# The first loads of a decode kernel: both halves of the gate weights at once, x behind them

## The chip, the cores and the metric

The kernel runs on one core of one Trainium2 chip. The metric is the device time of one execution in microseconds (us), as the median of several runs. A core has five engines that run side by side: TensorE (PE in the profile; PEld is its weight load), VectorE (DVE), ScalarE (ACT), GpSimd (POOL) and SyncE (SP). Loads from device memory (HBM) are issued by SP and by ACT, each into a queue of its own, and are moved by 16 DMA engines.

## The reference

One decode step of an attention block, gated by a gated linear unit, for 8 sequences with one token each (D = 512), 32 query heads, 8 key/value heads of 128, and a window of the last 2048 of 8192 cached positions. All inputs are bf16. The unit has F = 1792 hidden columns.

```python
def _A_ref(x, k_cache, v_cache, wq, wo):        # attention over the window
    W = min(4096, max(256, Sk // 4))             # 2048
    q = (x @ wq).reshape(B, Sq, Hq, Dh).transpose(0, 2, 1, 3)
    k = jnp.repeat(k_cache[:, :, Sk - W:, :], rep, axis=1)
    v = jnp.repeat(v_cache[:, :, Sk - W:, :], rep, axis=1)
    scores = jnp.einsum("bhqd,bhkd->bhqk", q, k) * (Dh ** -0.5)
    o = jnp.einsum("bhqk,bhkd->bhqd", _softmax(scores, axis=-1), v)
    return o.transpose(0, 2, 1, 3).reshape(B, Sq, Hq * Dh) @ wo

def _B_ref(x, w_gate, w_up, w_down):             # gated linear unit
    h = _sigmoid(x @ w_gate) * (x @ w_up)
    return h @ w_down

xn = _layernorm(A_x)
return A_x + _A_ref(xn, ...) * _silu(_B_ref(xn, ...))
```

## The kernel before, in words

The kernel reads some 81 MB, nearly all of it once. It has three stages: the gated unit and the queries at the start, the attention over 8 batch entries, and the output product at the end.

**Loads.** Two pools hold what arrives: `kpool` with 5 buffers and `vpool` with 4. A list `todo` gives the order of all loads: gate weights (`want_first`), up weights, down weights (one part of them in a tile `wd_part` of its own, L179 to L190, after the query weights), query weights in two tiles, then K tiles and V tiles of 2 MB each with V three tiles behind K, and last the output weights `wo` in five pieces. `pump` (L110) issues loads from the head of the list as long as the pool of the next one has room; `free` (L116) gives a buffer back and pumps again. Nearly all loads go to SP's queue (`q0`); ACT's queue (`q1`) gets one half of the gate weights and the small load of `x4_sb`. Each engine's instructions run in the order of the program, and a load's issue stands in that order too, so an issue that has to wait holds back all issues behind it.

**The first loads.** `want_first` (L147) issues three things. `x_bf` is x as 8 rows of 512 values, for the normalisation. The gate weights are one tile with four rows of `w_gate` for each partition; rows 0 and 1 go to ACT's queue, rows 2 and 3 to SP's. `x4_sb` is x once more, as four column blocks of 128 values in every fourth partition (32 pieces of 256 bytes); it is cleared by GpSimd at L144, and it is read once, at the very end (L750), where x is added to the result.

**The gated unit.** x is cast, its mean and variance are taken, and it is normalised (L223 to L236; the square root is on ACT), turned by TensorE (L247) and written to `xnT_sb` (L254). Then DVE clears and prepares other tiles (L259 to L280). TensorE multiplies with the gate weights (`hidden`, L295, 16 matmuls), ACT takes the sigmoid (L308), TensorE multiplies with the up weights (16 more), DVE forms the product `h_sb` (L312) and turns it (L320). The down product (L348) has 13 matmuls with `wd_sb` and 3 with `wd_part`. L357 to L375 sum its four blocks and form `gg_sb`, the gate's silu, with a sigmoid on ACT (L371).

**Queries and attention.** TensorE forms q with the query weights (L385); ACT and DVE copy it (L399, L401), and it is turned into `qm_sb`. From then on each K tile is turned on TensorE (L481), copied by DVE (L486) and multiplied with q (L500); maxima, exponentials (L548 on ACT), the turned probabilities (L571) and the products with V (L597) of earlier batch entries lie between. A K or V buffer is free, and the next load can be issued, when the last instruction that reads it is done.

**The end.** The output product (L719, L733) takes the pieces of `wo` as they land; DVE multiplies with `gg_sb` (L748) and adds `x4_sb` (L750), and SP and ACT store one half each (L752).

Of the kernel before, what the change touches and what calls it, by code (L numbers as in the profile page):

```python
# [10 lines left out]
def kernel(  # L11
# [14 lines left out]
    P = 128  # L26
# [54 lines left out]
    q0, q1 = nc.sync, nc.scalar  # L81
# [55 lines left out]
    x_bf = work.tile([B, D], bf16, name="x_bf")  # L137
# [3 lines left out]
    S = Z // B  # L141
    NB = D // P
    x4_sb = work.tile([P, P], bf16, name="x4_sb")
# [2 lines left out]

    def want_first():  # L147
        t = vpool.tile([P, KT, F], bf16, name="wg_sb", tag="v")
        q0.dma_start(out=x_bf[:], in_=A_x.flatten_outer_dims())
        for q, r0 in ((q1, 0), (q0, KT // 2)):  # L150
            q.dma_start(
                out=t[:, r0 : r0 + KT // 2, :],
                in_=B_w_gate.rearrange("(p r) n -> p r n", r=KT)[
                    :, r0 : r0 + KT // 2, :
                ],
            )
        q1.dma_start(
            out=x4_sb[::S, :],
            in_=A_x.flatten_outer_dims().rearrange("b (j c) -> j b c", c=P),
        )  # L160
        for r in range(KT):
            weights[("wg_sb", r)] = t[:, r, :]

    later("v", want_first)
    want_rows("wu_sb", B_w_up, "v", KT, 0, KT)

# [38 lines left out]
    for t0, t1 in ((0, 12), (12, KS), (KS, 26), (26, 30), (30, RT)):  # L205
# [11 lines left out]
        out=perm[:].rearrange("k (l p) -> k l p", l=G),  # L217
        in_=ident[:].rearrange("k (p l) -> k l p", l=G),
# [13 lines left out]
        out=rstd[:], in_=mv[:, 1:2], func=AF.Sqrt, bias=eps_t[:], scale=1.0  # L232
# [4 lines left out]
        out=xn_bf[:],  # L237
# [8 lines left out]
    for kt in range(KT):  # L246
        nc.tensor.transpose(  # L247
            out=xnT_ps[:, kt, :],
            in_=xn_bf[:].rearrange("b (p kt) -> b kt p", kt=KT)[:, kt, :],
# [11 lines left out]
    for t in p_buf:  # L261
# [7 lines left out]
        out=own_q[:], in_=ident_f[:].rearrange("k (h q) -> k q h", q=NDQ), axis=AX.X  # L269
# [3 lines left out]
        out=sel_z[:], in_=ident_f[:].rearrange("k (j z) -> k z j", z=Z), axis=AX.X  # L273
# [4 lines left out]
    for p0, n, x0, x1, s0, a in PARTS:  # L278
        for x in range(x0, x1):
            nc.vector.tensor_copy(  # L280
                out=sel_part[:, x, p0 : p0 + n].rearrange("k (a e) -> k a e", a=a),
                in_=ident[:, s0 : s0 + n * (x1 - x0)].rearrange(
                    "k (e x a) -> k x a e", x=x1 - x0, a=a
                )[:, x - x0],
# [6 lines left out]
    def hidden(name):  # L291
# [21 lines left out]
        out=h_sb[:].rearrange("k t p -> k p t"),  # L313
# [7 lines left out]
        out=hT_sb[:].rearrange("k t z -> k (t z)"),  # L321
        in_=h_sb[:].rearrange("k t p -> k (t p)"),
# [23 lines left out]
    for t, (h, w) in enumerate(down):  # L346
        j = t % NB
# [25 lines left out]
    free("v")  # L373
    gg_sb = work.tile([P, P], f32, name="gg_sb")
    nc.vector.tensor_tensor(out=gg_sb[:], in0=sigb[:], in1=b_ps[:], op=ALU.mult)  # L375

# [23 lines left out]
    for x in range(Hkv // JQ):  # L402
        for r in range(rep):
            nc.tensor.transpose(  # L404
                out=qT_ps[:, x, r, :], in_=q_bf[:, x, r, :], identity=ident[:]
            )
        nc.vector.tensor_copy(
            out=qm_sb[:, :, x * JQ : (x + 1) * JQ, M0 : M0 + rep],
            in_=qT_ps[:, x].rearrange("d r (j z) -> d z j r", z=Z)[:, ::S],
# [11 lines left out]
    for i in range(NQ):  # L421
        nc.vector.tensor_copy(
            out=turn_rows[:].rearrange("k (i j l r) -> k i j l r", i=NQ, j=NJ, l=G)[
                :, i
            ],
            in_=ident[:].rearrange("k (l j i r) -> k i j l r", i=NQ, j=NJ, l=G)[:, i],
        )
        nc.vector.reduce_sum(
            out=sel_den[:, i * Hh : (i + 1) * Hh].rearrange("k (l r) -> k l r", l=G),
            in_=ident_f[:].rearrange("k (l j i r) -> k i l r j", l=G, j=NJ, i=NQ)[:, i],  # L430
            axis=AX.X,
        )
    for e in range(2):
        nc.vector.reduce_sum(
            out=sel_out[:, e, :].rearrange("k (i h) -> k i h", i=NQ),
            in_=ident_f[:].rearrange(
                "k (i m e h) -> k e i h m", i=NQ, m=NJ // 2, e=2
            )[:, e],
# [9 lines left out]
        out=sel_res[:],  # L448
# [6 lines left out]
        out=sel_sum[:], in_=sel_den[:].unsqueeze(2).to_broadcast([P, Hq, NDQ])  # L455
# [261 lines left out]
    for t in range(KS):  # L717
        j = t % NB
# [32 lines left out]
    for x, q in enumerate((q0, q1)):  # L751
        q.dma_start(  # L752
            out=out.flatten_outer_dims().rearrange("b (j c) -> j b c", c=P)[
                x * NB // 2 : (x + 1) * NB // 2
            ],
            in_=y_bf[x * HP : (x + 1) * HP : S, :],
# [31 lines left out]
```

## Time and profile before

| | |
|---|---|
| median of 3 runs | 199.88 us (199.76 to 199.95) |
| the profiled execution | 199.75 us |
| its span, first to last instruction | 198.0 us |
| bytes read from HBM | 81.02 MB, 409 GB/s over the span |
| queue of SP (q1): packets, MB | 6224, 80.10 |
| queue of ACT (q10): packets, MB | 198, 0.93 |
| busy: PE, DVE, ACT, POOL | 155.6, 122.6, 37.7, 2.7 us |

All times in the profile count from the first instruction of the span. A row of the timeline gives start, duration, engine, line, operation, the tile written and the tile or tensor read; in brackets stands how long the engine was idle before it and what released it. "SPq" and "ACTq" are the issues of loads on the two queues; an issue is not the transfer, which comes later. The strip on the page cuts the span into 40 slices of 4.95 us; a digit is a busy share in tenths, 9 being 90% or more. The name `x_sb` in the profile is the tile `x4_sb` with its number left out. Windows give the busy time of each engine in a stretch of time, the granted clock of TensorE, the mean busy share of the 16 DMA engines (it can pass 1, since a packet counts where it starts) and the rate in GB/s.

### The profile page before, as it was taken

How to read it: one execution, taken by the hardware profiler on the slowest of the kernel's cores; microseconds unless marked ns; L12 is line 12 of the kernel's file. 1: busy time of each engine (PE TensorE's matmuls, PEld its weight loads, DVE VectorE, ACT ScalarE, POOL GpSimd, SP SyncE). 2: the span in 40 equal slices, each digit the busy share in tenths (PEclk: the TensorE clock that was granted, in tenths of full speed). 3: DMA queues.
4: the chain of work that ended last, by engine and by line, in shares of the span. 5: the costliest groups of instructions: out<-in, count | busy, mean ns of one | idle time of the engine just before them, and what ended most of it. 6: DMA issues, size and time to landing. Idle time of an engine off the chain costs nothing.

```text
span 198.0 us, 4774 instructions
## 1 busy us (share of the span) xinstructions
PE 155.6 (79%) x2133; PEld 105.6 (53%) x2133; DVE 122.6 (62%) x234; ACT 37.7 (19%) x91; POOL 2.7 (1%) x11
## 2 busy tenths in 40 slices
PE   0434038999979999999798869996999997888552
PEld 0111014877766677656565646674667665566421
DVE  3773001999978679758675927686767874852301
ACT  3300011000620520150024000600060033082010
POOL 5000000000000000000000000000000000000000
PEclk9999999999999999999999979997899999999985
DMA  6999999999999999999999999999999999999980
GB/s 209 446 430 434 426 425 427 434 440 429 424 420 430 430 427 437 430 430 420 430 427 425 427 440 430 422 434 424 424 430 440 420 430 437 427 420 425 420 336 10
DMA packets 6441, 81.32 MB, mean 411 GB/s; under 512 B 782, under 2 KB 918, under 8 KB 1558
## 3 DMA queue, kind: packets, MB, share of 16 engines
q1 hardware_dynamic: 6224, 80.10, 95.0%
q10 hardware_dynamic: 198, 0.93, 1.4%
q8 instruction: 16, 0.26, 0.5%
q14 instruction: 3, 0.02, 0.0%
HBM read 81.02 MB, written 0.01 MB: 409 GB/s over the span
## 4 chain that ended last, share of the span: by engine, by line
DMA 57%; PE 36%; ACT 3%; DVE 1%; SPq 1%; issue 1%
DMA k_sb<-in_A_k_cache_dram 32%; PE kT_ps L481 19%; DMA wo_sb<-in_A_wo_dram 11%; DMA wd_part<-in_B_w_down_dram 10%; PE o_ps L597 6%; PE s_ps L500 5%; DMA wg_sb<-in_B_w_gate_dram 3%; ACT p_buf L548 2%; PE pT_ps L571 2%; PE q_ps L385 1%; SPq L99 1%; ACT L548 1%; PE qT_ps L404 1%; PE fin_ps L733 1%; PE b_ps L361 0%
## 5 line engine op out<-in xcount | busy, mean ns | idle before, releaser
L486 DVE COPY kT_sb<-kT_ps 128x1024 bf16<-128x1024 bf16 x128 | 85.4, 687 | 30.2 <-PE kT_ps L481 29.5
L481 PE MATMUL kT_ps<-perm,k_sb 128*128 128x128 bf16 x1024 | 78.0, 225 | 8.2 <-DMA k_sb<-in_A_k_cache_dram 8.2
L481 PEld LDWEIGHTS <-k_sb 128*128 128x128 bf16 x1024 | 61.1, 101 | 28.0 <-issue 16.7
L597 PE MATMUL o_ps<-v_sb,pT_sb 128*32 128x256 bf16 x512 | 40.3, 279 | 1.2 <-DVE o_sb L618 0.9
L597 PEld LDWEIGHTS <-pT_sb 128*32 128x32 bf16 x512 | 22.1, 97 | 10.3 <-issue 3.8
L500 PE MATMUL s_ps<-kT_sb,qm_sb 128*32 128x512 bf16 x256 | 26.0, 396 | 0.7 <-DVE kT_sb L486 0.7
L548 ACT ACTIVATE p_buf<-s_ps,nb 32x512 bf16<-32x512 f32 x32 | 21.8, 680 | 0.5
L541 ACT COPY nb<-m_ps 128x1 f32<-128x1 f32 x8 | 1.3, 160 | 88.3 <-PE m_ps L535 88.3
L571 PE MATMUL pT_ps<-turn_rows,p_buf 128*128 128x128 bf16 x128 | 11.0, 230 | 1.5 <-ACT p_buf L548 1.5
L564 DVE COPY pT_sb<-pT_ps 128x1024 bf16<-128x1024 bf16 x14 | 9.6, 687 | 3.9 <-PE pT_ps L571 3.9
L571 PEld LDWEIGHTS <-p_buf 128*128 128x128 bf16 x128 | 9.4, 151 | 3.4 <-ACT p_buf L548 2.1
L500 PEld LDWEIGHTS <-qm_sb 128*32 128x32 bf16 x256 | 6.6, 93 | 7.7 <-issue 1.4
L613 ACT ACTIVATE o_odd<-o_ps,own_col 128x128 f32<-128x128 f32 x8 | 2.9, 368 | 26.8 <-PE o_ps L597 26.7
L375 DVE TENSOR_TENSOR gg_sb<-sigb,b_ps 128x128 f32<-128x128 f32 x1 | 0.3, 289 | 12.2 <-ACT sigb L371 12.2
L348 PE MATMUL w_ps<-wd_part,hP_sb 52*32 52x512 bf16 (+1 forms) x3 | 0.6, 597 | 8.3 <-DMA wd_part<-in_B_w_down_dram 8.3
L548 ACT ACTIVATION_READ_ACCUMULATOR p_buf<-s_ps,nb 32x1 f32 x32 | 5.9, 184 | 0.0
L515 DVE TENSOR_REDUCE st<-s_ps 128x1 f32<-128x512 f32 x8 | 5.5, 682 | 0.5 <-PE s_ps L500 0.5
L348 PEld LDWEIGHTS <-hP_sb 52*32 52x32 bf16 (+1 forms) x3 | 0.1, 98 | 9.2 <-issue 9.2
L247 PE MATMUL xnT_ps<-ident,xn_bf 8*128 8x8 bf16 x4 | 0.3, 174 | 5.8 <-DVE xn_bf L236 5.8
L640 DVE SCALAR_TENSOR_TENSOR own<-m_ps,inv,own_q 128x128 f32<-128x128 f32 x8 | 2.8, 345 | 3.1 <-PE m_ps L631 3.1
L618 DVE SCALAR_TENSOR_TENSOR o_sb<-o_ps,own_col,o_odd 128x128 f32<-128x128 f32 x8 | 2.7, 341 | 3.1 <-ACT o_odd L613 3.1
L295 PE MATMUL h_ps<-wu_sb,xnT_sb 128*32 128x448 bf16 x16 | 1.7, 572 | 3.4 <-DMA wu_sb<-in_B_w_up_dram 3.4
(80 smaller groups left out, 67.1 us busy)
## 6 DMA issues: line engine op xcount, KB each, us to landing
k_sb<-in_A_k_cache_dram SPq DMA_DIRECT2D x16, 2048.0 KB, 29.9
v_sb<-in_A_v_cache_dram SPq DMA_DIRECT2D x16, 2048.0 KB, 27.2
wq_sb<-in_A_wq_dram SPq DMA_DIRECT2D x2, 2048.0 KB, 19.9
wu_sb<-in_B_w_up_dram SPq DMA_DIRECT2D x1, 1792.0 KB, 10.3
wd_sb<-in_B_w_down_dram SPq DMA_DIRECT2D x1, 1664.0 KB, 13.8
wo_sb<-in_A_wo_dram SPq DMA_DIRECT2D x1, 1536.0 KB
wo_sb<-in_A_wo_dram SPq DMA_DIRECT2D x1, 1024.0 KB, 20.1
wg_sb<-in_B_w_gate_dram ACTq DMA_DIRECT2D x1, 896.0 KB
```

What stands on the lines that cost most here:

```text
L99: q0.dma_start(out=t[:], in_=w.rearrange("(p r) n -> p r n", r=per)[:, r0:r1, :])
L481: nc.tensor.transpose(out=kT_ps[:, c, :], in_=k_sb[:, j * CU + h * CH + c, :], identity=perm[:],)
L486: nc.vector.tensor_copy(out=kT[(b, u)][:, h * CH : (h + 1) * CH, :], in_=kT_ps[:])
L500: nc.tensor.matmul(s_ps[b][NR * l : NR * (l + 1), :], lhsT=qm_sb[:, b, i * G + l, o : o + Z], rhs=t[:, :, PG * l : PG * (l + 1)], start=(u ...
L515: nc.vector.reduce_max(out=st[b][:], in_=s_ps[b][:], axis=AX.X)
L548: nc.scalar.activation(out=p_buf[b % 2][rows, :, l, :], in_=s[rows, :].rearrange("k (c p) -> k p c", p=PG), func=AF.Exp, bias=nb[rows, :], ...
L564: copy(out=pT[b][:, h * CH : (h + 1) * CH, :], in_=pT_ps.pop(h)[:])
L571: nc.tensor.transpose(out=pT_ps[h][:, c, :], in_=p_buf[b % 2][:, :, :, h * CH + c].rearrange("k p l -> k (p l)"), identity=turn_rows[:],)
L597: nc.tensor.matmul(o_ps[rows, b % 2, :].rearrange("k (e d) -> k e d", e=2), lhsT=pT[b][:, c, rows], rhs=v[:, m, c], start=(c == 0), stop=( ...
L613: nc.scalar.mul(out=o_odd[:], in_=o_ps[:, b % 2, Dh:], mul=own_col[:, 1:2])
L618: nc.vector.scalar_tensor_tensor(out=o_of[b // 2][:, b % 2, :], in0=o_ps[:, b % 2, :Dh], scalar=own_col[:, 0:1], in1=o_odd[:], op0=ALU.mul ...
L640: nc.vector.scalar_tensor_tensor(out=own[:], in0=m_ps[:, b % 2, P : 2 * P].rearrange("p (q t) -> p q t", q=NDQ), scalar=inv[y][:, b % 2 : ...
```

## The change

`x_bf` and SP's half of the gate weights change places on SP's queue, so that the two halves are the first loads of the two queues. The load of `x4_sb` leaves the start of ACT's queue and is issued behind the gated unit, in the program's order after `gg_sb`; on ACT it stands behind the sigmoid of L371 and ahead of the copy of q. Nothing else is touched.

```diff
     def want_first():
         t = vpool.tile([P, KT, F], bf16, name="wg_sb", tag="v")
-        q0.dma_start(out=x_bf[:], in_=A_x.flatten_outer_dims())
         for q, r0 in ((q1, 0), (q0, KT // 2)):
             q.dma_start(
                 out=t[:, r0 : r0 + KT // 2, :],
                 in_=B_w_gate.rearrange("(p r) n -> p r n", r=KT)[
                     :, r0 : r0 + KT // 2, :
                 ],
             )
-        q1.dma_start(
-            out=x4_sb[::S, :],
-            in_=A_x.flatten_outer_dims().rearrange("b (j c) -> j b c", c=P),
-        )
+        q0.dma_start(out=x_bf[:], in_=A_x.flatten_outer_dims())
...
     gg_sb = work.tile([P, P], f32, name="gg_sb")
     nc.vector.tensor_tensor(out=gg_sb[:], in0=sigb[:], in1=b_ps[:], op=ALU.mult)
+
+
+    q1.dma_start(
+        out=x4_sb[::S, :],
+        in_=A_x.flatten_outer_dims().rearrange("b (j c) -> j b c", c=P),
+    )
```

## The prediction

> **What bounds the kernel now.** I read the page first (busy shares, the strip of 40 slices, the chain that ended last), then the windows of the first microseconds, the timeline of the gated unit, and the waits of the DMA-issuing queue. From the page:
>
> ```profile
> PE 155.6 (79%) x2133; PEld 105.6 (53%) x2133; DVE 122.6 (62%) x234; ACT 37.7 (19%) x91; POOL 2.7 (1%) x11
> ...
> DMA  6999999999999999999999999999999999999980
> ...
> DMA packets 6441, 81.32 MB, mean 411 GB/s; under 512 B 782, under 2 KB 918, under 8 KB 1558
> ...
> DMA 57%; PE 36%; ACT 3%; DVE 1%; SPq 1%; issue 1%
> ```
>
> The reader should see that TensorE has gaps (79%) and the DMA engines have none from the second slice to the last but two. 57% of the chain that ended last is DMA. The kernel is a single stream of 81.32 MB, and it ends when the stream ends plus a short tail. The same in windows of time; the columns are busy time of PE, PEld, DVE, ACT, POOL, then granted clock, DMA share and GB/s:
>
> ```profile
> 1.00:2.00 1.00, 0.00 (x0) 0.00 (x0) 0.00 (x0) 0.00 (x0) 1.00 (x1) 1.00 0.49 65
> 2.00:3.00 1.00, 0.00 (x0) 0.00 (x0) 0.21 (x1) 0.62 (x1) 0.86 (x5) 1.00 0.66 180
> 3.00:4.00 1.00, 0.00 (x0) 0.00 (x0) 0.75 (x3) 0.67 (x1) 0.41 (x2) 1.00 0.94 394
> 4.00:5.00 1.00, 0.00 (x0) 0.00 (x0) 0.60 (x4) 0.33 (x2) 0.00 (x0) 1.00 1.05 437
> ```
>
> From 40 to 160 us every window of 20 us shows 426 to 431 GB/s; I take 428. The stream is short of that rate only at its start: the engines' first data falls between 1.6 and 1.8 us, and by 4.0 us 65 + 180 + 394 = 639 KB have moved, which is 1.5 us of work at 428. Of the 2.3 us since 1.7, some 0.8 are lost in this ramp. That is all that a better start could win.
>
> The third view is the timeline of the first 30 us (start, duration, engine, line, what, idle before and its releaser):
>
> ```profile
> 0.73 0.41 SPq L149 DMA_DIRECT2D x_bf<-in_A_x_dram  x1
> 0.74 0.39 ACTq L151 DMA_DIRECT2D wg_sb<-in_B_w_gate_dram  x1
> ...
> 1.18 1.17 ACTq L157 DMA_DIRECT2D x_sb<-in_A_x_dram  x1
> 1.21 0.36 SPq L151 DMA_DIRECT2D wg_sb<-in_B_w_gate_dram  x1
> 1.61 0.43 SPq L99 DMA_DIRECT2D wu_sb<-in_B_w_up_dram  x1
> ...
> 3.23 0.46 DVE L223 CAST x_f<-x_bf 8x512 f32<-8x512 bf16 x1 [0.22 <-DMA x_bf<-in_A_x_dram]
> ...
> 7.65 0.94 PE L295 MATMUL h_ps<-wg_sb,xnT_sb 128*32 128x448 bf16 x8 [0.27 <-DMA wg_sb<-in_B_w_gate_dram]
> ...
> 13.74 2.08 DVE L312 TENSOR_TENSOR h_sb<-sig,h_ps 128x448 bf16<-128x448 f32 x1 [1.37 <-PE h_ps L295]
> ...
> 26.99 0.61 PE L348 MATMUL w_ps<-wd_part,hP_sb 60*32 60x512 bf16 x3 [8.32 <-DMA wd_part<-in_B_w_down_dram]
> ```
>
> The gated unit is ready early and TensorE then sits 8.32 us until wd_part has landed; this gap is the cover of everything that the change makes later. The last view is the queue that issues the loads:
>
> ```profile
> SPq L187 <- DMA wg_sb<-in_B_w_gate_dram: 1.7, 2, 1.3
> ...
> SPq L89 <- DMA x_sb<-in_A_x_dram: 0.4, 1, 0.4
> ```
>
> As the program is built, loads take eight completion semaphores in turn, so an issue can wait for an earlier landing. The first issue of wd_part starts at 5.44 in the timeline, after 1.3 us of waiting for ACT's half of the gate weights; TensorE resumes at 7.65 with SP's half; the first K load goes out at 8.71, when the column blocks (x4_sb, in the profile x_sb) have landed. Two halves issued 0.47 us apart (0.74 and 1.21) landed 2.2 us apart: the engines moved the one and then the other, not both in turn.
>
> **The change, part by part.** The profiled execution took 199.75 us, its span of 198.0 and 1.75 around it; the median of the three runs is 199.88, so it stands 0.13 below. The sum is made against 199.75.
>
> *The swap on SP's queue.* SP's half of the gate weights is issued at 0.73 instead of 1.21, and x_bf at about 1.1 instead of 0.73. The two issues (0.41 + 0.36) are the same two, so the load of the up weights (1.61) and all loads behind it keep their times. No bytes are added or removed. What can move is the ramp. Most it can give: the 0.8 us worked out above. Worst: in the window from 2 to 3 us the engines are busy for 0.66 of the time but move 0.42 of the full rate, so the first packets run slow, by 0.66 - 0.42 = 0.24 us in this window; from 1 to 2 us it is 0.49 - 0.15 = 0.34 us. If each queue pays such a slow start and the two add, the stream loses another 0.6 us. Between these ends I take a gain of 0.1 us: the stream is one stream already, its start is set by the issue at 0.73 in both kernels, and SP's half, once issued, stood behind ACT's in any case; what goes is the head start of eight 1 KB pieces of x on the engines, which precede the first weights.
> The Trainium skill, page "DMA: Bandwidth & Descriptors", section "Rules for kernel authors", says that loads put on several issuing queues run on the same 16 engines and gain no bandwidth, only issue time, and that two transfers to halves serialize. That speaks against the change. The landings at 5.4 and 7.6 agree with it; by the rule this term would be 0 and the sum 199.75.
>
> *x_bf later.* It now stands on SP's queue behind its half of the weights, with ACT's half on the same engines, so it lands when the halves have, about 7.5 us; it stands before the up weights, so the latest is their landing at 11.9 us (the next row of the timeline, the first matmul on wu_sb, starts at 11.94). The cast of x moves from 3.23 to 7.6. From the cast to xnT_sb in place took 3.15 us (3.23 to 6.38), so xnT_sb is there at 10.8. The 16 gate matmuls take 2 x 0.94, now without the pause for weights: 12.7. The 16 up matmuls (1.68) follow: 14.4. On ACT, the square root and the load of the sigmoid's table (1.28) end at about 10.6, before the sigmoid is wanted at 12.7. On DVE the clears, sums and copies of L259 to L280 stand behind xnT_sb in program order; they ran from 6.71 to 12.37, 5.7 us, and now run from 11.1 to 16.8. So h_sb starts at 16.8, not 13.74, and DVE is what is late next. Then 2.08 (h_sb), 0.65 (transpose), 0.3 for hP_ps and 1.9 for 13 matmuls of the down product: 21.8 us. The last three wait for wd_part until 26.99. Cover left: 5.2 us; with x landing at 11.9 it is still 0.8. Cost nothing. If that cover were gone, there is a second: TensorE's queries release the next K load, issued at 31.17, when 16.0 MB have been ordered (the sizes in the page's list of issues). The windows up to 10 us sum to 3.27 MB, 7.6 us at 428, so 2.4 are lost since the span's start, and 16.0 MB last until 2.4 + 37.4 = 39.8, 8.6 us after that issue.
>
> *Waits on SP's queue.* In the program as built, the semaphores turn by one place. The first piece of wd_part no longer waits for a landing; the other two wait for the gate halves, k of batch 0 for x_bf instead of the column blocks (7.5 instead of 8.4), the next two K loads for the down and the first query weights. The latest of these, a landing at 2.9 + 19.9 = 22.8, holds a load back while what is ordered before it (13.9 MB) lasts to 34.8. Cost nothing.
>
> *The column blocks of x.* Their issue (1.17 us on ACT) goes from 1.18 to behind the sigmoid that ends at 29.3. Queued behind it on ACT is the copy of q at 32.45, before which ACT idled 3.17 us: 1.17 fits, with 2.0 to spare. The 32 pieces of 256 B now share the engines with the K loads instead of the weights: the same bytes. Before, they landed 7.2 us after their issue; 29.3 + 7.2 = 36.5, and twice that is 43.7. They are read at 194.55. One V load waits for this semaphore in its turn; it was issued at 41.13, when 24.4 MB were ordered, enough until 59.4. Cost nothing. Leaving ACT's queue at the start lets its first table load go at 1.2 instead of 2.38, before a wait for the statistics: nothing.
>
> *Tail.* From the last landing of wo (TensorE resumes at 193.17) to the end nothing changes.
>
> Sum: 199.75 - 0.1 = 199.65, and as a median with part of the 0.13 between them, **199.7 us**. 0.2% (0.4 us) is about what a measurement of this kernel can tell from no change.
>
> **The rivals.**
> *The ramp closes (faster).* With weights waiting on both queues from the first moment, a slow first packet of one queue could run beside the other's, and the start would come nearer to 428 GB/s. For it: 0.66 busy at 180 GB/s is waiting, not moving. Against it: the two halves did not share the engines before. Half to all of 0.8 us: 198.95 to 199.35 in the sum, 199.1 to 199.5 as a median.
> *Each queue pays its slow start (slower).* Place: the engines' first packets, before 4 us. Price: up to 0.6 us, 200.35 in the sum, 200.5 as a median. It decides if the window from 1 to 4 us carries less than 639 KB by over 170 KB, that is 0.4 us at 428. For it: ACT's first packets ran slow although SP's queue had already moved x. Against it: the second half, which came last on SP's queue, ran at 437 GB/s from its first window.
> *x becomes the gate (slower).* It needs x to land after 12.7 us and then costs only once the lateness also eats the 8.6 us of loads on order. Its price then is a microsecond for each one beyond: 201 and up. Nothing in the profile puts x that late.
> *Nothing moves: the change doesn't do what it says.* The halves serialize as before and the start is the same: 199.75 in the sum, 199.9 as a median, so near the forecast that the two share one chance.
>
> **How the numbers follow.** The forecast, with nothing moving, 0.52, own range 199.5 to 200.1. The ramp closes by over 0.4 us: 0.31. Slower by over 0.4: 0.17, of which the double start 0.14 and x as the gate 0.03. The range for eight in ten reaches into the first rival to 199.0 and into the second to 200.4; what lies beyond is about a third of either. Faster 0.31, same 0.52, slower 0.17.
>
> **What the changed profile would show.** The cast of x at 7 to 8 us; h_sb near 16.8; the three wd_part matmuls still at about 27.0, after a wait of some 5 us instead of 8.32; the K load still issued near 31.2; ACT's column blocks near 29.3, the copy of q still at 32.4; DMA at 9 in all slices. The window from 1 to 4 us decides: 639 KB for no change, 810 KB or more for the first rival, 470 or less for the second. I am wrong if these hold and the end has moved by over 0.4 us all the same, which would mean that the stream's rate, not its start, depends on the order; or if wd_part is no longer what the down product waits for.

## The result, and the profile after

| | before | after |
|---|---|---|
| median of 8 runs each | 199.87 us (199.75 to 200.06) | 200.34 us (200.12 to 200.59) |
| ratio | | 1.0022, 95% interval 1.0012 to 1.0031 |
| the profiled execution | 199.75 us | 200.28 us |
| its span | 198.0 us | 198.5 us |
| last landing of `wo` | 193.39 us | 193.91 us |

The kernel became slower by 0.47 us, or 0.22%, and the interval lies clear of 1. The forecast was 199.7 with no change as the likeliest; its range held the time, its direction was wrong. The two landings in the last row are the last completion records of the DMA engines for the output weights: the 0.53 us between the two profiled executions is there (0.52) before the tail begins.

The page of the kernel after, the lines that answer to those shown of before:

```profile
PE 153.9 (78%) x2133; PEld 104.2 (52%) x2133; DVE 122.4 (62%) x234; ACT 37.6 (19%) x91; POOL 2.7 (1%) x11
...
DMA  6999999999999999999999999999999999999970
...
DMA packets 6441, 81.32 MB, mean 410 GB/s; under 512 B 782, under 2 KB 918, under 8 KB 1558
...
DMA 69%; PE 24%; DVE 2%; ACT 1%; SPq 1%; issue 1%
```

Packets and bytes are the same to the last digit, the strip of the DMA engines is full from the second slice to the last but two, and the chain of work that ended last is still a chain of transfers (69% DMA; it was 57%). Nothing has taken the stream's place as the bound. Its rate is not changed either: windows from 60 to 120 us have 429 GB/s (before 430), those from 120 to 180 us 429 (before 428). The windows of the start, in the same columns as before:

```profile
1.00:2.00 1.00, 0.00 (x0) 0.00 (x0) 0.00 (x0) 0.82 (x1) 1.00 (x1) 1.00 0.71 79
2.00:3.00 1.00, 0.00 (x0) 0.00 (x0) 0.22 (x1) 0.46 (x1) 0.86 (x5) 1.00 0.64 179
3.00:4.00 1.00, 0.00 (x0) 0.00 (x0) 0.01 (x1) 0.00 (x0) 0.41 (x2) 1.00 0.79 330
4.00:5.00 1.00, 0.00 (x0) 0.00 (x0) 0.00 (x0) 0.00 (x0) 0.00 (x0) 1.00 1.02 430
```

79 + 179 + 330 = 588 KB by 4 us, 51 KB less than the 639 before. At 428 GB/s that is 0.12 us of work, a quarter of what was lost. The window of 3 to 4 us shows it: the engines are busy for 0.79 of it, not 0.94. The timeline of the first 33 us:

```profile
0.73 0.39 SPq L150 DMA_DIRECT2D wg_sb<-in_B_w_gate_dram  x1
0.74 0.41 ACTq L150 DMA_DIRECT2D wg_sb<-in_B_w_gate_dram  x1
...
1.19 0.36 SPq L156 DMA_DIRECT2D x_bf<-in_A_x_dram  x1
1.59 0.36 SPq L99 DMA_DIRECT2D wu_sb<-in_B_w_up_dram  x1
...
7.80 0.41 DVE L219 CAST x_f<-x_bf 8x512 f32<-8x512 bf16 x1 [4.79 <-DMA x_bf<-in_A_x_dram]
...
10.68 0.23 DVE L250 COPY xnT_sb<-xnT_ps 128x32 bf16<-128x32 bf16 x1 [0.46 <-PE xnT_ps L243]
...
10.97 1.69 PE L291 MATMUL h_ps<-wg_sb,xnT_sb 128*32 128x448 bf16 x16 [0.40 <-DVE xnT_sb L250]
...
16.81 2.07 DVE L308 TENSOR_TENSOR h_sb<-sig,h_ps 128x448 bf16<-128x448 f32 x1
...
26.65 0.61 PE L344 MATMUL w_ps<-wd_part,hP_sb 60*32 60x512 bf16 x3 [4.92 <-DMA wd_part<-in_B_w_down_dram]
...
28.73 1.17 ACTq L374 DMA_DIRECT2D x_sb<-in_A_x_dram  x1
...
32.10 0.58 ACT L401 CAST q_bf<-q_ps 128x512 bf16<-128x512 f32 x1 [3.17 <-PE q_ps L387]
```

The two halves go out 0.01 us apart instead of 0.47. The gated unit runs 4.6 us later at the cast and 3.1 us later at `h_sb`, and is back in step at the three `wd_part` matmuls: they start at 26.65 (before 26.99) after a wait of 4.92 us that was 8.32. The copy of q still finds ACT idle for 3.17 us. The end of both kernels, first before, then after:

```profile
193.17 1.01 PE L733 MATMUL fin_ps<-wo_sb,oP_sb 128*32 128x128 bf16 x24 [0.39 <-DMA wo_sb<-in_A_wo_dram]
...
194.55 0.29 DVE L750 TENSOR_TENSOR y_bf<-prod,x_sb 128x128 bf16<-128x128 f32 x1
```

```profile
192.80 1.90 PE L735 MATMUL fin_ps<-wo_sb,oP_sb 128*32 128x128 bf16 x48
...
195.08 0.29 DVE L752 TENSOR_TENSOR y_bf<-prod,x_sb 128x128 bf16<-128x128 f32 x1
```

From the last landing to the end of `y_bf` it is 1.45 us before (193.39 to 194.84) and 1.46 after (193.91 to 195.37). So the tail only follows, and the loss lies somewhere between the first byte and the last landing.

**Where it lies: one engine's lateness.** The trace holds a record of every packet (start, duration, bytes, queue), and for each load a completion record of 4 bytes from each of the 16 DMA engines. The records do not name the engine; which packets belong to one engine was worked out by linking each packet to the one that starts where it ends, and gave 16 chains. Where two engines end a packet at the same moment such a chain can be mistaken; the completion records need no linking. The completion records of the gate weights stand at 6.46 to 7.28 us before. After, twelve engines are done by 7.21 and four only at 7.57 to 7.68. Those four keep their lateness: four of the 16 records of the first query weights stand at 20.65 to 20.76 with the rest at 20.29 or earlier (before, the last is at 20.40), and the last of `wo` is 0.53 us later at the end. It began with the first packets: a row of 7 KB takes 0.272 us in the steady stream; the first one of an engine took up to 1.15 us before, and 1.80, 1.78 and 1.77 us on three engines after. In this stream nearly every load gives each engine the same number of rows (8 of 128), so an engine that starts 0.5 us late has no chance to catch up, and TensorE waits until the last of the 16 engines has landed its rows. The mean over 16 engines, which a window in GB/s shows, hides that.

One thing more decides which of the late engines counts. The page of the profile lists 16 packets of instructions (queue q8, 0.26 MB), of 16 KB and 0.88 to 0.97 us each, between 33 and 186 us. In the chains of the kernel after they fall on eight of the engines, two on each, and with the packets that they slow put each of the eight some 2.9 us behind the others. So the engine that is last at the end is the latest one of these eight; of the four late engines of the kernel after, one fetches no instructions and is not among the last. Every kernel here has these 16 packets.

The Trainium skill, page "DMA: Bandwidth & Descriptors", section "Rules for kernel authors", says of two transfers to disjoint halves of the partitions that their packets are interleaved on the same 16 engines if two engines issue them. The halves here are halves of the rows, and each covers all 128 partitions; the chains of after show the same for them: packets of the two queues take turns, and both halves are complete at 7.67 and 7.68. In the kernel before, with 0.47 us between the issues, they do not take turns: the engines emptied ACT's half first (4.30 to 5.04) and then SP's (6.46 to 7.28).

### The profile page after: what moved, and what is told of

Read it like the earlier page. It is cut to its first block, busy times and chain, and to the rows that moved or that the text cites. A ratio compares the mean times of both kernels' runs of the same rounds, so it can differ in the third digit from the quotient of the medians.

```text
span 198.5 us, 4775 instructions
## 1 busy us (share of the span) xinstructions
PE 153.9 (78%) x2133; PEld 104.2 (52%) x2133; DVE 122.4 (62%) x234; ACT 37.6 (19%) x91; POOL 2.7 (1%) x11
## 4 chain that ended last, share of the span: by engine, by line
DMA 69%; PE 24%; DVE 2%; ACT 1%; SPq 1%; issue 1%
DMA k_sb<-in_A_k_cache_dram 47%; PE kT_ps L483 12%; DMA wo_sb<-in_A_wo_dram 10%; DMA wd_part<-in_B_w_down_dram 9%; PE o_ps L599 5%; DMA wg_sb<-in_B_w_gate_dram 4%; PE s_ps L502 3%; PE q_ps L387 1%; PE fin_ps L735 1%; DVE kT_sb L488 1%; PE part_ps L721 1%; PE qT_ps L406 1%; SPq L183 0%; PE b_ps L357 0%; PE w_ps L344 0%
## 5 line engine op out<-in xcount | busy, mean ns | idle before, releaser
L483 PE MATMUL kT_ps<-perm,k_sb 128*128 128x128 bf16 x1024 | 76.4, 223 | 9.8 <-DMA k_sb<-in_A_k_cache_dram 9.8
L483 PEld LDWEIGHTS <-k_sb 128*128 128x128 bf16 x1024 | 59.7, 99 | 29.9 <-issue 16.6
L371 DVE TENSOR_TENSOR gg_sb<-sigb,b_ps 128x128 f32<-128x128 f32 x1 | 0.3, 289 | 8.8 <-ACT sigb L367 8.8
```

What stands on the lines that cost most here:

```text
L483: nc.tensor.transpose(out=kT_ps[:, c, :], in_=k_sb[:, j * CU + h * CH + c, :], identity=perm[:],)
```

## The experiments

The theory after the result, R: the lateness of the slowest engine at the start is carried unchanged to the end, and the two halves at once make the first packets slow. The rivals: C, the chain behind the late x; X, the late load of `x4_sb`. Then, within R, what makes the first packets slow: H1, weights at the head of both queues; H2, no small load of x ahead of them; and H3, which came in only when f1 and f2 had spoken against the first two: the bytes that each engine is asked for in the first moment. All ratios are to the kernel before, run beside each.

**The parts apart.** One kernel has the change without the moved `x4_sb` load, one has that load alone moved.

```diff
 # e1: after, but
+        q1.dma_start(
+            out=x4_sb[::S, :],
+            in_=A_x.flatten_outer_dims().rearrange("b (j c) -> j b c", c=P),
+        )
         q0.dma_start(out=x_bf[:], in_=A_x.flatten_outer_dims())
...
-    q1.dma_start(
-        out=x4_sb[::S, :],
-        in_=A_x.flatten_outer_dims().rearrange("b (j c) -> j b c", c=P),
-    )
 # e2: before, with the same four lines moved from want_first to behind gg_sb
```

> The change without the moved load of the column blocks: x and SP's half of the gate weights change places, x4_sb stays at the start of ACT's queue. Theory R (the ramp): with gate weights at the head of both queues some DMA engines need longer for their first packets, and the latest engine keeps its lag to the end; expects ratio 1.0022 as for the whole change (200.3 us), with the windows from 1 to 4 us carrying some 590 KB instead of 639. Rival C (x late, the gated unit's chain): also 1.0022, but with the queries and the K stream's issues later than before. Rival X (the late load of x4_sb beside the K loads costs the 0.47 us): expects 1.000.

> The other part alone: x first on SP's queue as before, x4_sb issued behind the gated unit. Theory R and rival C: ratio 1.000 (199.9 us), ramp as before (639 KB from 1 to 4 us). Rival X: 1.0022.

Measured: the swap alone 200.43 us against 199.98, 1.0021 (1.0012 to 1.0030); the late column blocks alone 200.03, 1.0000 (0.9992 to 1.0009). The whole loss is in the swap, and X falls.

**The late x, or the start?** The gated unit can be made late without touching a single load: in the kernel before, the preparations of L259 to L280 (clears, sums, copies) are moved ahead of the cast of x on DVE.

```diff
+    qm_sb = work.tile([P, B, Hkv, M0 + Z], bf16, name="qm_sb")
+    nc.vector.memzero(qm_sb[:])
...
     nc.vector.tensor_copy(out=x_f[:], in_=x_bf[:])
...
-    qm_sb = work.tile([P, B, Hkv, M0 + Z], bf16, name="qm_sb")
-    nc.vector.memzero(qm_sb[:])
...
```

> The kernel before with its loads untouched; only DVE's clears, sums and copies (L259 to L280, 5.7 us) are moved ahead of the cast of x, so that the cast starts at 8.5 us and the gated unit is as late as after the change (7.8). Rival C (the late chain costs the 0.45 us): ratio 1.002, 200.4. Theory R (what matters is the lag of the latest DMA engine when the gate weights are in): 1.000, and the end 4.6 us behind the last landing as in the other kernels.

The timeline of that kernel:

```profile
8.93 0.41 DVE L253 CAST x_f<-x_bf 8x512 f32<-8x512 bf16 x1
...
12.09 1.69 PE L293 MATMUL h_ps<-wg_sb,xnT_sb 128*32 128x448 bf16 x16 [0.40 <-DVE xnT_sb L284]
...
27.22 0.61 PE L346 MATMUL w_ps<-wd_part,hP_sb 60*32 60x512 bf16 x3 [6.90 <-DMA wd_part<-in_B_w_down_dram]
```

The gate matmuls start at 12.09, later than the 10.97 of the changed kernel; with the preparations done, `h_sb` follows at 15.39 instead of 16.81, and TensorE still waits 6.90 us for `wd_part`. Measured: 199.77 against 199.79 us, 0.9999 (0.9990 to 1.0008). A gated unit that starts later costs nothing, and in the changed kernel, where its later steps are later still, TensorE waits 4.92 us for `wd_part` all the same. So C falls.

**x late in the old order, and x ahead in the new one.** One kernel is the kernel before with the x that is used loaded behind the halves, and an unread copy of it where x stood; the other is the kernel after with an unread load of x ahead of SP's half.

```diff
 # e3: before, but
-        q0.dma_start(out=x_bf[:], in_=A_x.flatten_outer_dims())
+        q0.dma_start(out=x_first[:], in_=A_x.flatten_outer_dims())   # read by nothing
...
+        q0.dma_start(out=x_bf[:], in_=A_x.flatten_outer_dims())
 # e4: after, but
+        q0.dma_start(out=x_first[:], in_=A_x.flatten_outer_dims())   # read by nothing
         for q, r0 in ((q1, 0), (q0, KT // 2)):
```

> The kernel before with x loaded twice: once at the head of SP's queue into a tile that nothing reads, and once behind the gate weights, which the normalisation uses. The start of the stream is that of before, the gated unit starts as late as after the change (cast of x at 7.5 to 8 us). Theory R: ratio 1.000 (199.9). Rival C: 1.0022 (200.3). Rival X: 1.000.

> The changed kernel with an 8 KB load of x, which nothing reads, put at the head of SP's queue, so that SP's half of the gate weights is issued 0.5 us behind ACT's again; the used x and x4_sb are as late as after the change. Theory R: ratio 1.000 (199.9), the two halves landing one after the other. Rival C and rival X: 1.0022 (200.3).

Measured: 200.31 against 199.98, 1.0020 (1.0011 to 1.0029), and 200.25, 1.0013 (1.0004 to 1.0021). R had expected 1.000 of both and missed. By these ratios alone, x late would have seemed to be the cause and x ahead no cure. The profiles say something else. `wo` has landed at 193.62 and 193.68, not at 193.9; but from the end of `y_bf` to the end of the span it is 3.44 and 3.39 us, where kernels without an extra load have 3.01 to 3.22. Both kernels have one load more than the others. So a later run put one more load where no start could be touched:

```diff
 # g1: before, but behind gg_sb
+    q1.dma_start(out=x_first[:], in_=A_x.flatten_outer_dims())       # read by nothing
```

> The kernel before with one more load of x (8 KB, into a tile that nothing reads) on ACT's queue behind the gated unit; the start is untouched. If one more load instruction lengthens the end of the program, as the three kernels that had one suggest: wo lands as before (193.4), the span after the last operation of VectorE is 3.4 to 3.5 instead of 3.1 to 3.2, and the ratio is 1.0013 (0.27 us). If the longer end of those three had to do with their starts: 1.000.

Measured: 200.17 against 199.84, 1.0016 (1.0008 to 1.0025), with `wo` landed at 193.37 as before, and 3.45 us behind `y_bf`. An added load of x thus cost some 0.33 us at the program's exit, wherever it stood in these kernels. Less that, the start of e3 costs 0.00 and that of e4 -0.06 us; with the intervals of the runs behind them, each of the two is uncertain by some 0.25 us (an estimate). The landings of `wo` in the two profiled executions, 0.23 and 0.29 us behind those of before, are about half of what the change lost. So x late is free as far as this pair can tell (e5 showed it better), and with SP's half issued 0.45 us after ACT's most of the loss is gone, if not all.

**The halves one after the other.** Both halves on SP's queue, x on ACT's; and the mirror image of before (SP: its half first, ACT: x, then its half). Both with the late `x4_sb`.

```diff
 # e6: after, but
-        for q, r0 in ((q1, 0), (q0, KT // 2)):
+        q1.dma_start(out=x_bf[:], in_=A_x.flatten_outer_dims())
+        for q, r0 in ((q0, KT // 2), (q0, 0)):
...
-        q0.dma_start(out=x_bf[:], in_=A_x.flatten_outer_dims())
 # e7: after, with the load of x_bf on q1 ahead of the loop, the loop untouched
```

> Both halves of the gate weights at the head of SP's queue, one behind the other; x alone at the head of ACT's queue, so that it is early again; x4_sb as after the change. Theory R leaves open whether the head of one queue is as bad as the heads of both: if the long first packets come from weights on both queues at once, 1.000; if they come from weights being the very first transfer on SP's queue, 1.002. Rival C: 1.000, since x is early.

> The kernel before mirrored: SP's half of the gate weights at the head of its queue, x at the head of ACT's and ACT's half behind it; x4_sb as after the change. Theory R as two queues at once: 1.000, since ACT's half starts 0.5 us behind. Theory R as weights first on SP's queue: 1.002. Rival C: 1.000.

Measured: 199.69 against 199.79, 0.9996 (0.9988 to 1.0005), and 199.72, 0.9999 (0.9991 to 1.0008). The loss is gone in both, and neither beats the kernel before by more than can be measured.

**All at once on one queue, ACT's half a little later, x ahead on both queues, and the change again.**

```diff
 # f1: after, but one load of all four rows
+        q0.dma_start(out=t[:], in_=B_w_gate.rearrange("(p r) n -> p r n", r=KT))
         q0.dma_start(out=x_bf[:], in_=A_x.flatten_outer_dims())
...
 # f2: after, SP as it is; ACT's half behind a square root of one column that nothing needs
...
+        nc.scalar.activation(out=one[:], in_=one[:], func=AF.Sqrt)
+        q1.dma_start(out=t[:, 0:2, :], in_=B_w_gate.rearrange("(p r) n -> p r n", r=KT)[:, 0:2, :])
 # f4: after, but on each queue x ahead of the half (ACT's copy read by nothing)
+        q0.dma_start(out=x_bf[:], in_=A_x.flatten_outer_dims())
+        q1.dma_start(out=x_first[:], in_=A_x.flatten_outer_dims())
         for q, r0 in ((q1, 0), (q0, KT // 2)):
...
-        q0.dma_start(out=x_bf[:], in_=A_x.flatten_outer_dims())
```

> The changed kernel with the gate weights as one load of 14 KB rows at the head of SP's queue, x behind it, nothing on ACT's queue at the start. Two readings of theory R are told apart: H1, long first packets come from gate weights at the head of both queues at once: 1.000 (as in the run with both halves on SP's queue). H2, they come from there being no small load of x ahead of the weights on any queue: 1.002.

> The changed kernel with ACT's half of the gate weights issued about 1.8 us later, behind a square root of a constant on ACT (which also brings its table load forward); SP's half first and x behind it as after the change. H1: 1.000, since only one queue has weights at the start. H2: 1.002, since no x goes ahead.

> Both halves issued at the same time, but half a microsecond later, each behind an 8 KB load of x at the head of its queue (the one on ACT's queue is read by nothing); x is early, x4_sb late. H1: 1.002, H2: 1.000.

> The changed kernel once more, beside the others on the same chip: 1.002. Its second profile should again show DMA engines whose first packet takes over 1.2 us, and the last piece of wo landing 186.2 us behind the last landing of the gate weights, as in the profiles so far; if the end moves without that landing, theory R is wrong.

| kernel | median, before 199.81 us | ratio |
|---|---|---|
| f1, one load of 14 KB rows | 200.19 | 1.0021 (1.0012 to 1.0030) |
| f2, ACT's half later | 199.74 | 0.9995 (0.9986 to 1.0004) |
| f4, x ahead on both | 200.65 | 1.0042 (1.0029 to 1.0054) |
| the change again | 200.28 | 1.0023 (1.0013 to 1.0032) |

The run f2 is the clearest. Its issues in the timeline, and its windows:

```profile
0.73 0.39 SPq L149 DMA_DIRECT2D wg_sb<-in_B_w_gate_dram  x1
...
1.01 0.39 ACTq L154 DMA_DIRECT2D wg_sb<-in_B_w_gate_dram  x1
1.19 0.36 SPq L150 DMA_DIRECT2D x_bf<-in_A_x_dram  x1
```

```profile
2.00:3.00 1.00, 0.00 (x0) 0.00 (x0) 0.19 (x1) 0.22 (x2) 0.86 (x5) 1.00 0.63 201
3.00:4.00 1.00, 0.00 (x0) 0.00 (x0) 0.04 (x1) 0.00 (x0) 0.44 (x2) 1.00 1.05 423
```

ACT's half goes out at 1.01 instead of 0.74 us. That is 0.27 us later and not the 1.8 that was expected: the issue did not wait for the square root, which ran at 2.03. Nothing else of the change is undone, x still stands behind the weights. From 3 to 4 us the stream runs at 423 GB/s (330 in the changed kernel), and the loss is gone; in the chains the engines take SP's half whole, and then ACT's. That ends H2: no x is ahead, and nothing is lost. The run f1 speaks against H1: one queue has all the weights, and the loss is there. f4 does not decide: its weights went out at 1.19 and 1.39, so not at the same time, and 0.46 us later than the change's; it has the exit of one more load (3.51 us); and these two account for most of its 0.84 us. The change again did what was expected of it: its longest first packet took 1.62 us, and the last `wo` landed 186.24 us behind the last record of the gate weights.

**The last two.** What was left, besides H3: f1 had neither x ahead nor small rows. So the one load was repeated with x alone at the head of ACT's queue; and the change with each half as two loads of one row of 3.5 KB for each partition, both queues still starting at once.

```diff
 # f5: f1, but
-        q0.dma_start(out=x_bf[:], in_=A_x.flatten_outer_dims())
+        q1.dma_start(out=x_bf[:], in_=A_x.flatten_outer_dims())
 # f6: after, but
-        for q, r0 in ((q1, 0), (q0, KT // 2)):
+        for r in range(2):
+            for q, r0 in ((q1, r), (q0, KT // 2 + r)):
...
-                out=t[:, r0 : r0 + KT // 2, :],
+                    out=t[:, r0 : r0 + 1, :],
```

> All gate weights as one load of 14 KB rows at the head of SP's queue, as in the run with one load, but x alone at the head of ACT's queue; the column blocks late; no instruction added. If what counts is how many weight bytes the engines are asked for in the first moment (14 KB for each partition): longest first packet 1.7 us or more, last wo landing near 193.9, ratio 1.002. If a load of x in front or beside the weights at the start is what keeps it fast: 1.000, last wo landing near 193.4, and the run with one load was slow only for want of it.

> The changed kernel with each half of the gate weights as two loads of one row (3584 B) for each partition, both queues issuing at once; two more load instructions. If the bytes asked for in the first moment count (2 x 3.5 KB instead of 2 x 7 KB): the latest engine is through the first query weights at 20.2 to 20.4 and wo has landed at 193.3 to 193.4; with the exit of the two more loads (0.27 us each, if the one below shows that) the median is at most 0.5 above before. If it is the two queues at the head that count, whatever the size: 20.6 to 20.9 and 193.7 to 194.0, median 0.7 to 1.0 above before.

Measured, against 199.84: f5 200.11, 1.0015 (1.0007 to 1.0024); f6 199.95, 1.0008 (1.0000 to 1.0017), with `wo` landed at 193.39 as in the kernel before and 3.25 us behind `y_bf`, so that its 0.11 us is mostly exit. The window from 3 to 4 us of f5, and then of f6:

```profile
3.00:4.00 1.00, 0.00 (x0) 0.00 (x0) 0.70 (x3) 0.00 (x0) 0.41 (x2) 1.00 0.82 344
```

```profile
3.00:4.00 1.00, 0.00 (x0) 0.00 (x0) 0.02 (x1) 0.00 (x0) 0.41 (x2) 1.00 1.04 416
```

Both came out as H3 has it. Two queues that start with weights at the same instant lose nothing if the rows are half as long (against H1), and a load of x beside the weights saves nothing if they are one load of 14 KB rows (against H2).

**All profiles together.** From the packet records of each profiled execution: the three longest packets of gate weights that started before 4.5 us, the time at which the latest of the 16 engines was through with the first tile of query weights, the last landing of `wo`, and the execution's time:

```text
kernel                first packets, us   query weights   last wo   execution
before                1.15 1.12 1.11          20.40        193.39     199.75
e5 late gated unit    1.02 0.90 0.89          20.62        193.48     199.75
e6 both on SP         1.24 1.18 0.89          20.18        193.32     199.62
e7 mirror             1.37 1.20 0.87          20.33        193.47     199.79
f2 ACT's half later   1.15 1.04 0.86          20.20        193.34     199.74
f6 quarters           0.87 0.87 0.86          20.28        193.39     199.82
g1 late extra load    1.23 1.20 0.76          20.23        193.37     200.07  (exit +0.3)
e3 late x             1.24 1.22 1.19          20.47        193.62     200.29  (exit +0.3)
e4 x ahead of SP's    1.50 1.41 1.40          20.53        193.68     200.33  (exit +0.3)
after                 1.80 1.78 1.77          20.76        193.91     200.28
after, again          1.62 1.62 1.52          20.58        193.74     200.07
e1 swap alone         1.94 1.91 1.54          20.92        194.07     200.49
f1 one load           1.98 1.91 1.36          20.70        193.86     200.15
f5 one load, x on ACT 1.99 1.94 1.43          20.83        193.98     200.22
e2 late x4_sb         1.19 1.17 1.06          20.87        194.01     200.41
f4 x ahead on both    1.46 1.42 1.20          20.85        193.96     200.70  (exit +0.3, issued late)
```

In 14 of the 16 the last `wo` lands 173.11 to 173.16 us after the query weights. That is R: 173 us of stream, in which the lateness of the last engine is kept, to 0.05 us. In the two exceptions (before 172.99, e5 172.86) it is another engine's record at 20 us that fits, 20.24 and 20.32, 0.16 and 0.30 ahead of the latest; the engine that was last then was not the last at the end. An engine that fetches no instructions would do that; in these two kernels it was not followed to the end. The row of e2 shows the same cause without the change: its profiled execution was the slowest of its 11 (median 200.03), and there one engine had two slow packets in a row, 1.17 and then 0.96 us. The kernels with the long first packets (1.6 us and more) are the four with 14 KB for each partition issued at one instant: after, e1, f1 and f5.

**An attempt to give the late engines less.** If the latest engine sets the end, dealing the rows unevenly might help. One tile of query weights was loaded as 112 rows on SP's queue and twice 8 rows on ACT's.

```diff
-    for i in range(2):
-        want_rows("wq_sb", A_wq, "k", KT, 2 * i, 2 * i + 2)
+    def want_uneven():
+        for q, p0, p1 in ((q0, 0, 112), (q1, 112, 120), (q1, 120, 128)):
+            q.dma_start(out=t[p0:p1], in_=src[p0:p1, 0:2, :])
...
```

> The kernel before with 16 of the 128 rows of the first tile of query weights (16 KB each) taken off the even split: 112 rows go as one load (7 rows for each of the 16 DMA engines by the split that the packets of the other loads show), and 16 rows as two loads of 8 rows on ACT's queue (one row each for 8 engines). Bytes are the same. In the packets of before, 8 engines end 1.2 to 3.4 us behind the other 8. Theory R says that the end is that of the latest engine: taking one row of 0.61 us from each of those gives 0.5 to 0.6 us, ratio 0.997 (199.4). A rival by which the summed rate of the stream decides: 1.000.

Measured: 212.31 against 199.79 us, 1.0621 (1.0602 to 1.0639); both forecasts, 0.997 and 1.000, missed. From the page, the rate in slices of 5.2 us, and from the waits of SP's queue:

```profile
GB/s 226 237 196 300 313 250 393 434 422 434 425 426 428 425 434 434 425 434 425 425 425 431 433 428 428 429 434 419 431 434 425 431 431 428 437 419 423 420 305 5
```

```profile
SPq L187 <- DMA wg_sb<-in_B_w_gate_dram: 6.8, 1, 6.8
...
SPq L187 <- DMA wu_sb<-in_B_w_up_dram: 5.4, 1, 5.4
```

The stream ran at 196 to 313 GB/s in the second to the sixth slice; the 16 KB packets of the 8-row loads took 0.71 to 1.95 us instead of 0.61, and the packets of the other loads beside them were slowed too. The gate weights landed so late that SP's queue waited 6.8 us for them and issued the first piece of `wd_part` only at 13.29, and the three `wd_part` matmuls came at 38.95. The two loads of 8 rows also went out at 2.38 and 2.74 us, since nothing held ACT's queue back, and ran among the gate and up weights instead of beside the rest of their tile. So the attempt says nothing on whether the late engines could be unloaded, and which part of it cost the 12.5 us stays open.

## Why the prediction was wrong, and where it was right

**The swap on SP's queue: wrong.** This is the step that failed. The term was taken as -0.1 us between -0.8 and +0.6. It measured +0.45 (e1 against before), in the range, with the other sign. That the measured time lies in the stated range is owed to the second rival, whose price had widened it, and not to this term. Three of its points failed:

- "SP's half, once issued, stood behind ACT's in any case." It did when it was issued 0.47 us later. Issued at the same moment, the two take turns packet by packet, and the engines are asked for twice as much at once.
- "what goes is the head start of eight 1 KB pieces of x" was counted as a gain. In the old order the issue of x (0.41 us on SP) had kept the second half back, and this was worth 0.45 us. f2 gets it back with 0.28 us between the two issues, without x ahead.
- The ramp was priced as a mean rate over 16 engines. By that price the change lost 51 KB, 0.12 us. What counts is the slowest engine, 0.4 us late at 7.7 us and 0.5 us later than before at the end. f1 shows how little the mean says: by 4 us it has moved 143 + 201 + 344 = 688 KB, 49 more than before, and it lost 0.38 us (its 14 KB packets count whole where they start, which flatters the sum).

**The rival "each queue pays its slow start": right place, sign and size, wrong test.** It named the engines' first packets before 4 us and a price of up to 0.6 us, and had a chance of 0.14. Its criterion was that the window from 1 to 4 us carry less by over 170 KB; it carried less by 51, and the rival came true all the same. As the prediction set it up, 588 KB would have been read as a small start cost, and the 0.5 us at the end as a sign that "the stream's rate, not its start, depends on the order". The rate after the start is the same to 1 GB/s (429 and 430), so that reading would have been wrong too. The mechanism as named, a slow start that each queue pays, was also not right: f1 and f5 lose 0.38 and 0.27 us with all weights on one queue, and f6 starts with weights on both and loses nothing at the landing.

**The rival "the ramp closes": wrong.** From 3 to 4 us the rate fell from 394 to 330 GB/s instead of rising.

**x_bf later: right.** Forecast and measured: cast of x 7.6 and 7.80; `xnT_sb` 10.8 and 10.68; end of the gate matmuls 12.7 and 12.66; `h_sb` 16.8 and 16.81; end of the 13 down matmuls 21.8 and 21.73; the wait for `wd_part` 5.2 and 4.92 us. It cost nothing, as forecast; e5, later still up to the gate matmuls, shows it by itself.

**Waits on SP's queue: right in the sum, not in the piece.** The chain of semaphores turned as described. The first piece of `wd_part` went out at 3.98 without a wait, and the second then stood 3.2 us for a half of the gate weights:

```profile
SPq L183 <- DMA wg_sb<-in_B_w_gate_dram: 3.2, 1, 3.2
```

The first K load followed at 9.70 instead of 8.71, and the fourth at 30.82 instead of 31.17. The rates from 4 to 10 us are 439 GB/s in both kernels, so none of this was felt.

**The column blocks of x: right.** Issued at 28.73 (forecast 29.3), landed at 37.0 to 37.5 (36.5), read at 195.08; e2 gives 1.0000.

**The tail: right**, 1.46 us against 1.45 from the last landing to the end of `y_bf`.

## What to carry to other kernels

In this kernel, one long stream of loads that are dealt evenly to all DMA engines, the end was set by an engine that was late from the start, so a change of the first loads is judged by the latest completion records and not by the mean rate. 14 KB for each partition asked of idle engines at one instant, on two queues or on one, lost 0.27 to 0.47 us here; 0.28 us between the issues of the two halves, or rows half as long, avoided it. And a probe that adds an instruction has a price of its own: measure it by a control that adds the same instruction where it can do no harm.

## What was not expected of the hardware

- The first packet of an engine took 0.27 to 1.99 us for what takes 0.27 (7 KB) or 0.54 us (14 KB) in the stream. The longest was 1.62 to 1.99 us with 14 KB for each partition issued at one instant, 1.02 to 1.50 us with two halves of 7 KB issued at least 0.2 us apart, and 0.87 us with quarters of 3.5 KB. What in the path to memory does it stays open, and f6 does not tell shorter rows from fewer bytes in the first 0.4 us. The Trainium skill, page "DMA: Bandwidth & Descriptors", section "Latency and other measured facts", gives the latency of HBM as 0.2 us on average and 2 us at high load; the measured first packets lie between the two, and no run here shows whether that is the cause.
- The section "Rules for kernel authors" of the same page of the Trainium skill advises one load of all 128 partitions instead of two loads of half the partitions. No run here tests that, since each half of the gate weights covers all 128 partitions. The prediction read the row as one on these halves and had 0 from it for the swap, which measured +0.45 us. What the runs show beside it is that for the first load of this kernel one load measured 1.0021 (f1) and 1.0015 (f5), and two halves of the rows 0.28 us apart 0.9995 (f2): how the first load is split was not free.
- A lag of 0.5 us of one engine is still there after 173 us of full stream, to 0.05 us.
- The 16 fetches of instructions put eight of the DMA engines some 2.9 us behind the other eight in the kernel after, so the lateness of those eight decides the end.
- One more small load of x, wherever it stands, lengthened the exit behind the last operation of VectorE from 3.01 to 3.22 us to 3.39 to 3.51 us (e3, e4, f4, g1); two more loads of weights in f6 did less (3.25). The reason is open.
- A tile loaded as 112 + 8 + 8 rows, the last two ahead of their turn on ACT's queue, cost 12.5 us.
